# Attention with decay and a feed-forward layer on one core: the places of operands in on-chip memory

## The chip, the core and the metric

The kernel runs on one core of a Trainium2 chip. The core has engines that work beside each other: TensorE (PE) multiplies matrices and writes to PSUM, VectorE (DVE) and ScalarE (ACT) do elementwise work and move data between PSUM and the on-chip memory SBUF, GpSimd (POOL) fills tables, and SyncE (SP) issues the transfers (DMAs) here. They wait for each other by semaphores. A product on PE has two instructions: a load of the stationary operand (the weights, 128x128; rows of the profile call it PEld), and the matmul proper, which streams the moving operand through.

The metric is the time of one execution on the device, in microseconds. The median of three runs of the kernel before is 647.0 us (646.7 to 647.45).

## The reference

Two layers, all in float32. The first is attention with decay over 4 batches, 8 heads, 768 positions of 64 features, computed in blocks with a state that is carried on:

```
intra = (q_b k_b^T) * Dmask          # Dmask[i,j] = lam^(i-j) where i >= j, else 0
out   = intra v_b + (q_b * lam^(i+1)) kv_state
kv_state = lam^block * kv_state + (k_b * lam^(block-1-j))^T v_b
```

Its output, 3072 tokens of 512 features, goes through a feed-forward layer:

```
h   = maximum(x @ w_in, 0)           # 512 -> 2048
out = (h * h) @ w_out                # 2048 -> 512
```

## The kernel before

*Tiles.* The 24 chunks of 128 positions (4 batches, 6 chunks each) are grouped three at a time into eight tiles of 384 tokens. For each tile and each of 16 blocks f of 128 hidden features, `ffn` (L498) does one step. The first product (`mm1`, L507) multiplies x by a block of w_in: 12 matmuls of 384 columns. ACT takes the relu (L521); the square is taken on ACT alone for the first two tiles (L523, L524), on ACT and DVE for the others (L526, L527); DVE makes the low part gl (L528). The second product (`mm2`) has nine matmuls of 512 columns: six at L513 and L514 with gh, three at L516 with gl.

*Two parts of a number.* Where the products run on the type float32r, a value is held as a high part and a low part, each of that type: xh and xl, wih and wil, woh and wol, gh and gl, and a product is the sum of three. In the first product the stationary operand is wih or wil and the moving one xh or xl. In the second gh or gl is stationary, in pieces of 128 columns, and woh or wol moves.

*Attention.* The chunks of the first three tiles go through `unit_plain` (L302): products in float32 from tiles pnt. The others go through `unit_split` (L380): products in float32r, with operands ab, ka, ss, vv and pp made from tiles pkt by ACT and DVE. Plain work ends before split work begins: the buffers of the plain chunks and of the preparation of weights (kinds in `EARLY`, L154) are given back, and the buffers in `LATE` are laid over the same memory (`late`, L209).

*What sets the order.* Nothing is scheduled at run time. Every operation is entered with `plan.op`: its engine, an assumed duration in microseconds, a key, and what it depends on. `Plan.order` plays all engines through with these durations and so writes out one order for each engine; each engine then works through its list and waits on semaphores. The durations of the products stand at L518, L530, L531 and L537. SP is one such list too: loads of pnt, of weights (L276), of pkt (L401) and the stores (L549).

*Where the buffers lie.* SBUF tiles are allocated one after the other (L191 to L207), each rounded up to 32 bytes of a partition. Counted in rows of 512 bytes, all buffers from gh to xl1 begin 128 bytes into a row, since their sizes are whole rows and small constants stand before them. Then come five small tables, lam, ej, ec, wdec and lc (L194 to L198), which take 64 + 32 + 32 + 32 + 32 = 192 bytes. So everything behind them, rdec, mask, all weights, and the early and late buffers, begins 320 bytes into a row. lam holds the decays, wdec and lc their powers, ej and ec the exponents; they are filled at the start (`start_tables`, L221), and flip, a table for one product at the start, already lies in the first 128 columns of the last g buffer.

## Time and profile before

| what | value |
|---|---|
| median of three runs | 647.0 us (646.7 to 647.45) |
| profiled execution, its own time | 646.68 us |
| its span, first to last instruction | 644.9 us |
| mean granted clock of TensorE | 0.999 |
| PE busy | 635.6 us (99%) |
| weight loads (PEld) busy | 569.3 us (88%) |
| DVE busy | 470.9 us (73%) |
| ACT busy | 372.4 us (58%) |
| POOL busy | 5.5 us (1%) |

The profiled execution is one run with the hardware profiler on. Busy times of different engines overlap, so they don't add up to the span. Matmuls are pipelined: each shows a length of 337 ns (384 columns) or 395 to 400 ns (512 columns), while the next one starts long before that has passed, so the distance from start to start says more than the length. In the timeline, equal instructions that follow each other are merged into one row with a count. Idle time in brackets is that of the engine before the row, and behind the arrow stands what ended it.

### The profile page before, as it was taken

The numbers are of one execution on the slowest core, as the hardware profiler recorded it, in microseconds if no ns is written. First come the engines' busy times: TensorE is split into PE (matmuls) and PEld (weight loads), VectorE is DVE, ScalarE is ACT, GpSimd is POOL, SyncE is SP. The second block draws the span as 40 slices with busy tenths as digits, with TensorE's granted clock in tenths as the row PEclk, the third lists the DMA queues.
The fourth block names the chain that finished last, engine by engine and source line by source line (L and its number), as shares of the span: only waits on it lengthen the run. The fifth ranks groups of instructions, "written<-read, shape, count | busy, mean of one in ns | idle before, by whom it ended". The sixth has DMA issues, their size and how long they took to land.

```text
span 644.9 us, 9615 instructions
## 1 busy us (share of the span) xinstructions
PE 635.6 (99%) x3620; PEld 569.3 (88%) x3620; DVE 470.9 (73%) x1046; ACT 372.4 (58%) x863; POOL 5.5 (1%) x15
## 2 busy tenths in 40 slices
PE   8999999999899999999999999999999999999997
PEld 6788989888789998899989999899899898999996
DVE  4999999744348998589975999759995798742222
ACT  6996777755445666366654657556664567532221
POOL 2000000000000000000000000000000000000000
PEclk9999999999999999999999999999999999999999
DMA  7725555430221221231202122121130121010001
GB/s 290 266 99 180 181 189 201 164 115 10 91 85 62 66 90 42 99 99 49 99 1 98 55 94 98 50 100 49 50 99 33 67 99 50 1 50 1 0 1 49
DMA packets 15165, 56.71 MB, mean 88 GB/s; under 512 B 1808, under 2 KB 1808, under 8 KB 15120
## 3 DMA queue, kind: packets, MB, share of 16 engines
q1 hardware_dynamic: 15120, 56.11, 25.4%
q8 instruction: 28, 0.46, 0.3%
q14 instruction: 17, 0.14, 0.1%
HBM read 49.81 MB, written 6.29 MB: 87 GB/s over the span
## 4 chain that ended last, share of the span: by engine, by line
PE 82%; DVE 13%; ACT 3%; DMA 1%; issue 1%; SPq 0%; ACTq 0%
PE h L507 35%; PE bank L516 13%; PE bank L513 12%; PE bank L514 12%; PE bank L473 2%; PE bank L472 2%; PE bank L430 2%; DVE xr L485 1%; DVE g L527 1%; PE bank L450 1%; PE bank L317 1%; DVE gl L528 1%; DVE s L438 1%; PE bank L369 1%; DVE ka L418 1%; DVE ab L416 1%
## 5 line engine op out<-in xcount | busy, mean ns | idle before, releaser
L513 PE MATMUL bank<-woh,gh 128*128 128x512 f32 x384 | 152.1, 396 | 0.0
L514 PE MATMUL bank<-wol,gh 128*128 128x512 f32 x384 | 151.6, 395 | 0.0
L521 ACT ACTIVATE g<-h 128x384 f32<-128x384 f32 x128 | 62.8, 491 | 128.6 <-PE h L507 128.4
L516 PE MATMUL bank<-woh,gl 128*128 128x512 f32 x384 | 111.7, 400 | 0.6 <-DVE gl L528 0.2
L507 PE MATMUL h<-xh,wih 128*128 128x384 f32 x512 | 110.3, 337 | 1.8 <-ACT g L521 1.8
L527 DVE TENSOR_TENSOR g<-g 128x384 f32<-128x384 f32 x96 | 53.5, 557 | 79.5 <-ACT gh L526 79.1
L507 PE MATMUL h<-xh,wil 128*128 128x384 f32 x512 | 109.8, 336 | 0.0
L507 PE MATMUL h<-xl,wih 128*128 128x384 f32 x512 | 109.4, 336 | 0.0
L507 PEld LDWEIGHTS h<-xh,wih 128*128 128x128 f32 x512 | 89.8, 188 | 6.6 <-ACT g L521 2.2
L507 PEld LDWEIGHTS h<-xh,wil 128*128 128x128 f32 x512 | 90.6, 188 | 0.0
L507 PEld LDWEIGHTS h<-xl,wih 128*128 128x128 f32 x512 | 90.4, 188 | 0.0
L516 PEld LDWEIGHTS bank<-woh,gl 128*128 128x128 f32 x384 | 70.1, 188 | 19.5 <-DVE gl L528 4.1
L513 PEld LDWEIGHTS bank<-woh,gh 128*128 128x128 f32 x384 | 72.2, 188 | 13.4 <-issue 0.2
L514 PEld LDWEIGHTS bank<-wol,gh 128*128 128x128 f32 x384 | 72.2, 188 | 13.1
L528 DVE TENSOR_TENSOR gl<-g,gh 128x384 fp32r<-128x384 f32 x128 | 71.1, 556 | 16.7 <-ACT gh L524 13.5
L526 ACT ACTIVATE gh<-g 128x384 fp32r<-128x384 f32 x96 | 50.5, 526 | 2.5
L479 ACT COPY z<-bank 128x256 f32<-128x256 f32 x60 | 22.3, 372 | 38.4 <-PE bank L473 35.9
L480 DVE TENSOR_TENSOR z<-bank,z 128x256 f32<-128x256 f32 x60 | 25.0, 423 | 14.1 <-ACT z L479 12.7
L473 PE MATMUL bank<-pp,vv 128*128 128x256 f32 x120 | 29.8, 281 | 0.0
L472 PE MATMUL bank<-ab,ss 128*128 128x256 f32 x120 | 29.7, 281 | 0.0
L437 ACT COPY s<-bank 128x256 f32<-128x256 f32 x60 | 20.0, 373 | 14.2 <-PE bank L430 13.9
L485 DVE TENSOR_TENSOR xr<-z,zl 64x256 f32<-64x256 f32 x60 | 25.1, 418 | 2.0 <-ACT zl L481 1.0
(78 smaller groups left out, 775.1 us busy)
## 6 DMA issues: line engine op xcount, KB each, us to landing
pkt<-pk SPq DMA_DIRECT2D x30, 768.0 KB, 4.4
st<-w SPq DMA_DIRECT2D x32, 512.0 KB, 3.4
pnt<-pn SPq DMA_DIRECT2D x18, 512.0 KB, 4.5
out<-ob SPq DMA_DIRECT2D x23, 256.0 KB, 2.2
out<-z SPq DMA_DIRECT2D x1, 256.0 KB, 2.0
lam<-lamx SPq DMA_DIRECT2D x1, 6.0 KB, 1.7
```

Source lines behind the costliest of these rows:

```text
L472: nc.tensor.matmul(y4[:, n], at(ss)[:, n, h].rearrange("p t d -> p (t d)"), at(ab)[:, i], start=n == 0, stop=False, skip_group_check=True)
L473: nc.tensor.matmul(y4[:, n], at(vv)[:, i].rearrange("p t d -> p (t d)"), at(pp)[:, i], start=False, stop=True, skip_group_check=True)
L480: zo.append(add("DVE", 0.36, 2, lambda h=h, part=part: nc.vector.tensor_tensor(out=at(z)[:, h], in0=part(0), in1=at(z)[:, h], op=ALU.add), ...
L485: nc.vector.tensor_tensor(out=at(xr)[half(h)], in0=at(z)[0:64, h], in1=at(zl)[:, h], op=ALU.add)
L507: nc.tensor.matmul(at(h)[:, 0:N], wt[:, cc, :], xt[:, cc, :], start=k == 0, stop=k == 3 * NCC - 1)
L513: nc.tensor.matmul(at(os_[j]), at(gh)[:, sl], woh[f], start=f == 0, stop=False)
L514: nc.tensor.matmul(at(os_[j]), at(gh)[:, sl], wol[f], start=False, stop=False)
L516: nc.tensor.matmul(at(os_[j]), at(gl)[:, sl], woh[f], start=False, stop=f == NF - 1)
L521: orr = plan.op("ACT", 0.45, key, lambda: nc.scalar.activation(at(g), at(h)[:, 0:N], AF.Relu), [o1], [h, g])
L526: ogh = plan.op("ACT", 0.47, key, lambda: nc.scalar.activation(at(gh), at(g), AF.Square), [orr], [g, gh])
L527: og = plan.op("DVE", 0.48, key, lambda: nc.vector.tensor_tensor(out=at(g), in0=at(g), in1=at(g), op=ALU.mult), [orr, ogh], [g])
L528: ogl = plan.op("DVE", 0.48, key, lambda: nc.vector.tensor_tensor(out=at(gl), in0=at(g), in1=at(gh), op=ALU.subtract), [og, ogh], [g, gh, gl])
```

## The change

The tables lam, ej and ec move into unused columns of the last g buffer (from column 128 on, behind flip). wdec and lc move behind the weights. So rdec, mask and all weights begin 128 bytes into a row, as the buffers before them do. wdec and lc take 64 bytes, so the early buffers begin at 192. The late pool starts with a tile `space` of 448 bytes, and the late buffers begin at 128 again. In the planner the durations of the products are written anew, the list of plain chunks is written by its count of chunks (nine, the same chunks), and one start key changes for tiles of which none is split (no effect).

```diff
-N_PLAIN = 3
-PLAIN = [bc for t in TILES[:N_PLAIN] for bc in t]
-SPLIT = [bc for t in TILES[N_PLAIN:] for bc in t]
+N_PLAIN = 9
+PLAIN, SPLIT = CHUNKS[:N_PLAIN], CHUNKS[N_PLAIN:]
...
-    lam = const.tile([P, 12], F32, name="lam")
-    ej = const.tile([P, H], F32, name="ej")
-    ec = const.tile([P, NP], F32, name="ec")
-    wdec = const.tile([P, H], F32, name="wdec")
-    lc = const.tile([P, NP], F32, name="lc")
     rdec = const.tile([P, NP, C], F32, name="rdec")
 
     flip, zero = tiles["g"][-1][:, 0:P], tiles["ob"][-1]
+    lam, ej, ec = (tiles["g"][-1][:, P + 16 * i:P + 16 * i + n] for i, n in enumerate((H + NP, H, NP)))
...
+    wdec = const.tile([P, H], F32, name="wdec")
+    lc = const.tile([P, NP], F32, name="lc")
     make(phase.enter_context(tc.tile_pool(name="early", bufs=1)), EARLY)
 
     def late():
         phase.close()
-        make(ctx.enter_context(tc.tile_pool(name="late", bufs=1, reuse_waits="tile")), LATE)
+        pool = ctx.enter_context(tc.tile_pool(name="late", bufs=1, reuse_waits="tile"))
+        pool.tile([P, 112], F32, name="space")
+        make(pool, LATE)
...
-        o1 = plan.op("PE", 2.09, key, mm1, list(ready) + list(wo[0]), [x, h], [last_mm.get((ti, 1))])
+        o1 = plan.op("PE", 2.085, key, mm1, list(ready) + list(wo[0]), [x, h], [last_mm.get((ti, 1))])
...
-            o2 = plan.op("PE", 1.41, key + 1.9, lambda: [mm2(0, j) for j in range(NT)], [ogh] + list(wo[1]), [gh] + os_, [last_mm.get((ti, 2))])
-            last_mm[ti, 2] = o3 = plan.op("PE", 0.7, key + 1.9, lambda: [mm2(1, j) for j in range(NT)], [ogl], [gl, gh] + os_, [o2])
+            o2 = plan.op("PE", 1.37, key + 1.9, lambda: [mm2(0, j) for j in range(NT)], [ogh] + list(wo[1]), [gh] + os_, [last_mm.get((ti, 2))])
+            last_mm[ti, 2] = o3 = plan.op("PE", 0.685, key + 1.9, lambda: [mm2(1, j) for j in range(NT)], [ogl], [gl, gh] + os_, [o2])
...
-                elif ti < N_PLAIN:
+                elif (b, c) in PLAIN:
...
-                    f0 = 0.5 if ti > 2 else 2.0
+                    f0 = 0.5 if ti > 2 else 1.0
```

The new durations make the planner write another order. Two engines are shown at the place where plain chunks end and split ones begin, and POOL at the start. In the names the number behind the last underscore is a running number of the tile and shifts by itself; the number before it is the buffer.

PE before, from the last product of a plain chunk with the state (L366) on; woh10 is the second weight block of step 10, wih11 to wih13 the first ones of the steps that follow:

```order
L366 MATMUL bank2_63<-pnt1_174,diag1_0_179 128x128 x2
L369 MATMUL bank2_63<-s1_1_89,vd1_91 64x128 x4
L516 MATMUL bank1_62<-woh10_148,gl1_73 128x512
L516 MATMUL bank0_61<-woh10_148,gl1_73 128x512
L516 MATMUL bank5_66<-woh10_148,gl1_73 128x512
L507 MATMUL h1_68<-xh1_97,wih11_117 128x384 x4
L507 MATMUL h1_68<-xl1_98,wih11_117 128x384 x4
L507 MATMUL h1_68<-xh1_97,wil11_133 128x384 x4
L507 MATMUL h0_67<-xh1_97,wih12_118 128x384 x4
L507 MATMUL h0_67<-xl1_98,wih12_118 128x384 x4
L507 MATMUL h0_67<-xh1_97,wil12_134 128x384 x4
L507 MATMUL h1_68<-xh1_97,wih13_119 128x384 x4
```

PE now, from the same product on:

```order
L366 MATMUL bank2_63<-pnt1_171,diag1_0_176 128x128 x2
L369 MATMUL bank2_63<-s1_1_89,vd1_91 64x128 x4
L513 MATMUL bank1_62<-woh11_144,gh0_69 128x512
L514 MATMUL bank1_62<-wol11_160,gh0_69 128x512
L513 MATMUL bank0_61<-woh11_144,gh0_69 128x512
L514 MATMUL bank0_61<-wol11_160,gh0_69 128x512
L513 MATMUL bank5_66<-woh11_144,gh0_69 128x512
L514 MATMUL bank5_66<-wol11_160,gh0_69 128x512
L516 MATMUL bank1_62<-woh11_144,gl0_72 128x512
L516 MATMUL bank0_61<-woh11_144,gl0_72 128x512
L516 MATMUL bank5_66<-woh11_144,gl0_72 128x512
L513 MATMUL bank1_62<-woh12_145,gh2_71 128x512
```

Before, three second products and then the first products of steps 11, 12 and 13 follow. Now the nine second products of step 11 and the nine of step 12 come next, and after them the first products of steps 13 and 14 and then the second ones of step 13; the first products of steps 11 and 12 stand ahead of the L366.

ACT before, at the first casts from pkt to ab (L415); L521 is the relu, and the first one behind the casts takes the h of step 11:

```order
L521 ACTIVATE g2_77<-h0_67 128x384
L523 ACTIVATE g2_77<-g2_77 128x384
L524 CAST gh1_70<-g2_77 128x384
L375 CAST xh0_95<-xr0_93 128x2x128
L375 CAST xh0_95<-xr1_94 128x2x128
L415 CAST ab0_1646<-pkt0_1644 128x4x128
L417 CAST ka0_1648<-pkt0_1644 128x512
L406 CAST ss0_0_1653<-hold0_80 64x2x64 x2
L415 CAST ab1_1647<-pkt1_1645 128x4x128
L521 ACTIVATE g0_75<-h1_68 128x384
L422 CAST vv0_1649<-vd0_90 128x4x64
L523 ACTIVATE g0_75<-g0_75 128x384
```

ACT now, at the same casts; the first relu behind them takes the h of step 13:

```order
L521 ACTIVATE g1_76<-h0_67 128x384
L523 ACTIVATE g1_76<-g1_76 128x384
L524 CAST gh2_71<-g1_76 128x384
L375 CAST xh0_95<-xr1_94 128x2x128
L415 CAST ab0_1670<-pkt0_1668 128x4x128
L417 CAST ka0_1672<-pkt0_1668 128x512
L406 CAST ss0_0_1677<-hold0_80 64x2x64 x2
L415 CAST ab1_1671<-pkt1_1669 128x4x128
L422 CAST vv0_1673<-vd0_90 128x4x64
L406 CAST ss1_0_1678<-hold1_81 64x2x64 x2
L521 ACTIVATE g0_75<-h1_68 128x384
L523 ACTIVATE g0_75<-g0_75 128x384
```

The casts from pkt stand two steps later among the relus, and the cast to vv and the second pair to ss now stand ahead of the relu.

POOL at the start, before and then now, with what each instruction waits for:

```order
L229 AFFINE_SELECT g_77<-g_77 128x128 [waits DVE_49]
L230 AFFINE_SELECT mask<-mask 128x128 [waits DVE_49]
L233 MEMSET diag_0_177 128x256
L233 MEMSET diag_1_178 128x256
L233 MEMSET diag_0_179 128x256
L233 MEMSET diag_1_180 128x256
L235 TENSOR_TENSOR wdec<-lam,ej 128x8 [waits DMAHW0_49,Pool_49]
```

```order
L229 AFFINE_SELECT g_77<-g_77 128x128 [waits DVE_49]
L230 AFFINE_SELECT mask<-mask 128x128 [waits DVE_49]
L233 MEMSET diag_0_174 128x256
L233 MEMSET diag_1_175 128x256
L233 MEMSET diag_0_176 128x256
L233 MEMSET diag_1_177 128x256
L235 TENSOR_TENSOR wdec<-g_77 128x8 [waits DMAHW0_49,Pool_49]
```

The sequence and the waits are the same; pow (L235) reads lam and ej out of g.

## Rows read from the trace of the kernel before

**Rows 1.** The page: busy time, share of the span, instructions.
```profile
PE 635.6 (99%) x3620; PEld 569.3 (88%) x3620; DVE 470.9 (73%) x1046; ACT 372.4 (58%) x863; POOL 5.5 (1%) x15
```

**Rows 2.** Table by stretch: stretch, length, busy time by engine, granted clock, DMA.
```profile
80.00:120.00 40.00, 40.00 (x202) 36.04 (x201) 39.55 (x79) 31.55 (x66) 0.53 (x1) 1.00 0.63 215
...
200.00:240.00 40.00, 40.00 (x228) 36.72 (x226) 37.11 (x89) 25.62 (x60) 0.00 (x0) 1.00 0.23 79
...
560.00:600.00 40.00, 40.00 (x205) 35.95 (x204) 14.86 (x28) 11.51 (x23) 0.00 (x0) 1.00 0.06 20
```

**Rows 3.** Waits: who waited for whom, us in total, times, longest.
```profile
PEld bank L516 <- DVE gl L528: 4.1, 11, 0.6
...
PE h L507 <- ACT g L521: 1.8, 1, 1.8
```

**Rows 4.** Timeline of PE late in the kernel: start, length, instruction.
```profile
578.03 0.39 PE L513 MATMUL bank<-woh,gh 128*128 128x512 f32 x1
...
580.13 0.39 PE L513 MATMUL bank<-woh,gh 128*128 128x512 f32 x1
...
582.23 0.86 PE L507 MATMUL h<-xh,wih 128*128 128x384 f32 x4
...
586.39 0.39 PE L513 MATMUL bank<-woh,gh 128*128 128x512 f32 x1
```

**Rows 5.** Groups by line: shapes and count, busy time and mean ns, idle.
```profile
L514 PE MATMUL bank<-wol,gh 128*128 128x512 f32 x384 | 151.6, 395 | 0.0
...
L507 PE MATMUL h<-xh,wih 128*128 128x384 f32 x512 | 110.3, 337 | 1.8 <-ACT g L521 1.8
...
L514 PEld LDWEIGHTS bank<-wol,gh 128*128 128x128 f32 x384 | 72.2, 188 | 13.1
```

**Rows 6.** Timeline, all engines, a second product and the next load.
```profile
636.55 0.39 PE L513 MATMUL bank<-woh,gh 128*128 128x512 f32 x1
636.56 0.19 PEld L514 LDWEIGHTS bank<-wol,gh 128*128 128x128 f32 x1
```

**Rows 7.** Timeline of PE in split attention: its value products.
```profile
240.77 0.28 PE L472 MATMUL bank<-ab,ss 128*128 128x256 f32 x1
...
241.71 0.39 PE L513 MATMUL bank<-woh,gh 128*128 128x512 f32 x1
```

**Rows 8.** Groups by line on ACT: three casts of 512 columns.
```profile
L441 ACT CAST pp<-s 128x512 fp32r<-128x512 f32 x30 | 18.6, 621 | 12.2 <-DVE s L439 11.7
...
L415 ACT CAST ab<-pkt 128x512 fp32r<-128x512 f32 x30 | 18.7, 624 | 3.3 <-DMA pkt<-pk 3.3
...
L286 ACT CAST woh<-m 128x512 fp32r<-128x512 f32 x16 | 9.9, 621 | 5.1 <-DVE m L284 4.9
```

**Rows 9.** Timeline, all engines, at the start.
```profile
0.80 0.38 SPq L222 DMA_DIRECT2D lam<-lamx  x1
...
3.20 1.64 POOL L235 TENSOR_TENSOR wdec<-lam,ej 128x8 f32<-128x8 f32 x1
```

**Rows 10.** Timeline, all engines, from plain to split chunks.
```profile
158.82 0.60 PE L366 MATMUL bank<-pnt,diag 128*128 128x128 f32 x4
...
159.50 0.81 SPq L401 DMA_DIRECT2D pkt<-pk  x2
...
159.95 0.96 PE L516 MATMUL bank<-woh,gl 128*128 128x512 f32 x3
...
163.94 0.62 ACT L415 CAST ab<-pkt 128x512 fp32r<-128x512 f32 x1 [3.01 <-DMA pkt<-pk]
...
165.84 0.62 ACT L415 CAST ab<-pkt 128x512 fp32r<-128x512 f32 x1 [0.24 <-DMA pkt<-pk]
...
166.37 0.48 ACT L521 ACTIVATE g<-h 128x384 f32<-128x384 f32 x1
...
166.90 0.96 PE L507 MATMUL h<-xh,wih 128*128 128x384 f32 x4 [1.83 <-ACT g L521]
...
168.10 0.51 ACT L524 CAST gh<-g 128x384 fp32r<-128x384 f32 x1
```

More of the change, by code (lines that the diff above doesn't have):

```diff
@@ L536, in ffn @@
             for j in range(NT):
-                o3 = plan.op("PE", 0.7, key + 1.9 + j * 0.01, lambda j=j: [mm2(0, j), mm2(1, j)], [ogh, ogl] + list(wo[1]), [gh, gl] + os_[j:], [o3])
+                o3 = plan.op("PE", 0.69, key + 1.9 + j * 0.01, lambda j=j: [mm2(0, j), mm2(1, j)], [ogh, ogl] + list(wo[1]), [gh, gl] + os_[j:], [o3])
                 done.append(o3)
```

## The prediction

> **What bounds the kernel now.** I read the page's busy times first: TensorE (PE) is busy 99% of the span, DVE 73%, ACT 58% [rows 1]. A busy PE is not yet a PE at its peak, so I went on to the table by stretch. [...] DVE fills 39.55 of 40 us while weights are prepared and 37.11 of 40 where chunks of attention are made beside the products, and only 14.86 of 40 near the end [rows 2]. Then the waits, for who holds PE up: PE itself waited 1.8 us for h, and its weight loads 4.1 us for gl, in 644.9 us [rows 3]. So the time is the number of products times the distance from one to the next, and the change can act on that distance.
>
> I took the distances from the late stretch, where nothing but the two large products runs. From 582.23 to 586.39 PE starts two groups of 12 first products (L507): 4.16 us / 24 = 173.3 ns each. From 578.03 to 580.13 it starts nine second products (L513, L514, L516): 2.10 us / 9 = 233.3 ns each [rows 4]. [...]
>
> **The change part by part.**
>
> *Places.* Each product reads two things at a time: the moving operand, and the weights of the next product. The load for L514 starts at 636.56, right behind the matmul of L513 at 636.55 [rows 6]. Before, the moving x of a first product lies 128 bytes into a row of 512 and the weights that load beside it (wih, wil) 320 bytes in; in a second product it is the other way round (woh, wol at 320, gh, gl at 128). After the change all six lie at 128. [...]
>
> [...]
>
> [...] The planner's costs (L518, L530, L531) say what a group of products takes. Before they are 2.09 for 12 first products, 1.41 for six second ones and 0.70 for three; the rows give 2.08, 1.40 and 0.70 [rows 4]. So these three entries are durations to within 0.01 us. The change writes 2.085, 1.37 and 0.685. That they are again durations, those of the new places, is an assumption, for no run shows it. If they are: 0.005 us + 0.04 us + 0.015 us less in each of 1536 / 12 = 128 groups [rows 5], so 0.6 us from the first products and 5.1 + 1.9 = 7.0 us from the second. I take 7.6 us. [...]
>
> [...]
>
> *Other readers of these tiles.* ACT writes 128x512 in 621 ns both to woh at 320 and from s at 128 to pp at 320, 624 ns from pkt to ab [rows 8]. So an ACT operand's place shows at most 3 ns. On the 863 instructions of ACT [rows 1] that is 2.6 us of an engine that is busy 58% of the span, which PE covers. I take ACT, and DVE and the transfers by the same measure, at zero; uncovered it would be 2.6 us to either side. The plain chunks' operands (pnt) go from 320 to 192, still beside vd and s1 at 128: zero.
>
> *Tables in g.* lam, ej and ec now lie in the last g buffer. The order shows the same waits on POOL, and the first steps keep their place: pow runs at 3.20 us, after lam was issued at 0.80 [rows 9]. The region has its next writer only when relu fills that g, long after. Zero, both ways, since the same instructions wait for the same transfers.
>
> *The late buffers.* pkt1 now also lies over the old pnt3, so its load waits for one more transfer. That one landed before the plain products that read it, and they all stand ahead of the L366 for which both loads wait anyway. Behind it on SP stand the stores of the second tile, whose buffers are filled later still. Zero.
>
> *The order at the hand-over.* With new costs the planner writes another order. Before, both loads of pkt are issued at 159.50, behind the last plain product (L366, 158.82). ACT reaches the cast of pkt, finds nothing, and sits idle 3.01 us until 163.94. The relu for h stands behind two casts to ab, one to ka and two to ss, and starts only at 166.37. PE has run out of h buffers: it waits 1.83 us and goes on at 166.90 [rows 10]. In the new order two more relus stand ahead of the casts, and the last L366 is followed by 18 second products and 24 first ones before PE needs the gh that is made behind the casts. From L366's end at about 159.4 on the old clock that is 0.5 (to the L516 at 159.95) + 18 x 0.233 + 24 x 0.173 = 8.9 us. ACT has the same pieces to do as before between the first cast of pkt and the cast to that gh (two casts to ab, one to ka, two groups to ss, one to vv, relu, square, cast to gh), only in another sequence. Before, that cast to gh starts at 168.10 and takes 0.51 [rows 10]: 9.2 us after the same point. So PE waits some 0.4 us, with what it takes to pass the word on, instead of 2.2 (that gap counted from matmul to matmul). Gain 1.8 us; ends: 2.2 if the wait goes, -0.5 if ACT is later still.
>
> *The order elsewhere* shifts which group stands beside which. The waits that can change there are the 4.1 us of weight loads for gl [rows 3]. Part of those stay hidden under the running matmul. I take zero, with 1.5 us to either side.
>
> **Sum.** On the profiled execution (646.68 us, span 644.9, so 1.8 around it): 646.68 - 7.6 - 1.8 = 637.3. The median of the runs is 0.3 above the profiled one, so 637.6 us. DVE stays under PE: where it is busy 37.11 of 40 us, 40 becomes about 39.4. In the stretch with 39.55 of 40 [rows 2] cover is thin. There the new order has PE's own work on the second tile to fill gaps. If DVE holds that stretch to its old length, 80 us x 1.2% = 1 us of the gain is lost, which is inside the range.
>
> **The rivals.**
> [...]
> *Places don't matter.* The distances stay at 173.3 and 233.3 ns and only the order moves: 647.0 - 1.8 = 645.2, between 643.5 and 647.5. [...] This covers the case that the change does not do what it says. [...]
> *The same place is worse.* [...] It decides from a mean loss of 0.67 ns a product on (1.8 us / 2688), say first products at 174.5 ns with the second unchanged. Against it: the planner's new costs are lower.
> *The new order waits.* The hand-over gets longer (+0.5) and new gl waits cost 1.5 us, while the products gain as forecast: 647.0 - 7.6 + 2.0 = 641.4.
>
> **How the numbers follow.** Forecast 0.62 (its own range 634.5 to 641); new order waits 0.08; one amount for each load 0.12; places don't matter 0.08; worse 0.10. A measurement here tells 0.2%, 1.3 us, from no change. Faster: 0.62 + 0.08 + 0.12, and 0.04 of the case that places don't matter: 0.86. Same: its other 0.04. Slower: 0.10. The range leaves out "worse" but for its mild half, and the lower half of the one-amount case: 631.0 to 648.0.
>
> **What would show it.** In the late stretch, where no order enters, I look for 12 first products in 2.08 us or 2.07, nine second ones in 2.05 instead of 2.10. If the second products stay at 233 ns, the term of the places is wrong and only the order moved. [...] At the hand-over: PE's gap near 165 us shrinks to under 1 us and moves behind the first products of step 14. POOL's pow still at 3.2 us would confirm the tables. A gap in PE before 120 us that was not there would mean that DVE's cover is gone.

## The result, and the profile after

The changed kernel takes 641.34 us (median of four runs, 640.98 to 641.44); the kernel before took 646.93 in the same set. The ratio is 0.9911, with a 95% interval of 0.9894 to 0.9929. A second set gives 641.21 us and 0.9903 (0.9887 to 0.9918). The forecast was 637.6: the sign was right and the time lies inside the whole range (631.0 to 648.0), but just outside the range of the forecast's own account (634.5 to 641), and 3.7 us of the forecast gain of 9.4 did not come.

The 47 executions of the kernel before that ran beside the versions below lie in two groups, 25 from 646.5 to 647.8 us and 22 from 648.1 to 649.0; the mean granted clock of TensorE is 0.999 or 1.000 in the first group and 0.996 or 0.997 in 20 of the 22 others. A profile with the same order shows below where the clock falls. The profiled run of [rows 1 to 10] is of the first group, and sums start from it.

The busy times and the chain of waits on the page of the changed kernel:

```profile
PE 631.4 (99%) x3620; PEld 569.4 (89%) x3620; DVE 469.4 (73%) x1046; ACT 372.1 (58%) x863; POOL 5.5 (1%) x15
...
PE 93%; ACT 3%; DMA 2%; issue 0%; DVE 0%; SPq 0%; ACTq 0%
```

Beside [rows 1] PE has 4.2 us less of busy time and the other engines did the same work. PE is still the bound, now for 93% of the chain.

The late stretch, TensorE's timeline of the changed kernel, answers to [rows 4]:

```profile
573.04 0.39 PE L513 MATMUL bank<-woh,gh 128*128 128x512 f32 x1
...
575.12 0.39 PE L513 MATMUL bank<-woh,gh 128*128 128x512 f32 x1
...
577.16 0.87 PE L507 MATMUL h<-xh,wih 128*128 128x384 f32 x4
...
579.27 0.85 PE L507 MATMUL h<-xh,wih 128*128 128x384 f32 x4
...
581.35 0.39 PE L513 MATMUL bank<-woh,gh 128*128 128x512 f32 x1
```

The row at 579.27 is where the second dozen of first products begins. The first nine second products after the turn from 384 to 512 columns take 2.08 us (231.1 ns each), the next nine 2.04 (226.7 ns). The first products, which took 2.08 us a dozen before, take 2.11 in the dozen behind a turn and 2.08 in the next. Two steps, 18 and 24 products, take 8.31 us where before took 8.36 (578.03 to 586.39). So both lengths lose something after each turn, and I had counted on the settled distance all along.

The hand-over, answering to [rows 10]: the timeline of the changed kernel, SP's queue, ACT and PE:

```profile
164.06 0.81 SPq L401 DMA_DIRECT2D pkt<-pk  x2
...
168.47 0.62 ACT L415 CAST ab<-pkt 128x512 fp32r<-128x512 f32 x1 [2.96 <-DMA pkt<-pk]
...
171.93 0.49 ACT L521 ACTIVATE g<-h 128x384 f32<-128x384 f32 x1
...
172.25 0.86 PE L507 MATMUL h<-xh,wil 128*128 128x384 f32 x4
...
173.01 0.51 ACT L524 CAST gh<-g 128x384 fp32r<-128x384 f32 x1
...
173.57 0.50 PE L513 MATMUL bank<-woh,gh 128*128 128x512 f32 x1 [0.47 <-ACT gh L524]
```

ACT stands at the cast of pkt as long as before (2.96 us against 3.01), and its relu (171.93) still comes behind all the casts, but PE has 18 second and 24 first products to do meanwhile. Its gap from matmul to matmul was 2.17 us and is 0.81, behind the first products of step 14 and not ahead of them, as forecast.

What I had set at zero and was not zero are the weight loads that wait for gl. The waits of the weight loads in the changed kernel:

```profile
PEld bank L516 <- DVE gl L528: 2.7, 11, 0.4
```

Before, they were 4.1 us [rows 3]. Five of these waits stand out before, near 250, 327, 406, 483 and 542 us, with gaps of 496 to 548 ns between the matmuls, one for each tile of split attention; none of the five is in the changed kernel. The timeline of the kernel before at the first of them, DVE, the first second product and the load that waits:

```profile
248.08 0.56 DVE L527 TENSOR_TENSOR g<-g 128x384 f32<-128x384 f32 x1
248.44 0.39 PE L513 MATMUL bank<-woh,gh 128*128 128x512 f32 x1
248.56 0.42 DVE L420 TENSOR_TENSOR vd<-pkt,wdec 128x256 f32<-128x256 f32 x1
...
248.89 0.68 DVE L442 TENSOR_TENSOR pp<-s,pp 128x512 fp32r<-128x512 f32 x1
...
249.49 0.55 DVE L528 TENSOR_TENSOR gl<-g,gh 128x384 fp32r<-128x384 f32 x1
...
250.10 0.53 PEld L516 LDWEIGHTS bank<-woh,gl 128*128 128x128 f32 x3 [0.54 <-DVE gl L528]
```

And the same place in the changed kernel:

```profile
246.03 0.56 DVE L527 TENSOR_TENSOR g<-g 128x384 f32<-128x384 f32 x1
...
246.51 0.68 DVE L442 TENSOR_TENSOR pp<-s,pp 128x512 fp32r<-128x512 f32 x1
...
247.11 0.55 DVE L528 TENSOR_TENSOR gl<-g,gh 128x384 fp32r<-128x384 f32 x1
...
247.58 0.42 DVE L420 TENSOR_TENSOR vd<-pkt,wdec 128x256 f32<-128x256 f32 x1
247.72 0.53 PEld L516 LDWEIGHTS bank<-woh,gl 128*128 128x128 f32 x3 [0.25 <-DVE gl L528]
```

Before, the product of pkt and a table (L420) stands between the square and gl, so gl ends after the sixth second product has begun, and PE stops. Now it stands behind gl. This holds for the first four of the five. At the fifth L420 stood behind gl already, and the square began late (540.39, against the L513 at 540.36); there the new order has PE do two products of the split attention ahead of those with gl, which fills the wait:

```profile
537.14 0.39 PE L430 MATMUL bank<-ab,ka 128*128 128x256 f32 x2
```

### The profile page after: what moved, and what is told of

It reads as the page before. It is cut to its first block, busy times and chain, and to the rows that moved or that the text cites. A ratio compares the mean times of both kernels' runs of the same rounds, so it can differ in the third digit from the quotient of the medians.

```text
span 639.6 us, 9612 instructions
## 1 busy us (share of the span) xinstructions
PE 631.4 (99%) x3620; PEld 569.4 (89%) x3620; DVE 469.4 (73%) x1046; ACT 372.1 (58%) x863; POOL 5.5 (1%) x15
## 4 chain that ended last, share of the span: by engine, by line
PE 93%; ACT 3%; DMA 2%; issue 0%; DVE 0%; SPq 0%; ACTq 0%
PE h L507 41%; PE bank L516 14%; PE bank L513 14%; PE bank L514 14%; PE bank L473 2%; PE bank L430 2%; PE bank L472 2%; PE bank L450 2%; DMA pnt<-pn 2%; DMA pkt<-pk 1%; PE bank L317 1%; PE bank L369 1%; ACT vd L328 1%; ACT diag L356 1%; PE bank L340 0%
## 5 line engine op out<-in xcount | busy, mean ns | idle before, releaser
L513 PE MATMUL bank<-woh,gh 128*128 128x512 f32 x384 | 151.1, 394 | 0.7 <-ACT gh L524 0.7
L521 ACT ACTIVATE g<-h 128x384 f32<-128x384 f32 x128 | 62.9, 492 | 139.3 <-PE h L507 138.9
L516 PE MATMUL bank<-woh,gl 128*128 128x512 f32 x384 | 110.4, 396 | 0.0
L527 DVE TENSOR_TENSOR g<-g 128x384 f32<-128x384 f32 x96 | 53.4, 557 | 75.7 <-ACT gh L526 75.2
L516 PEld LDWEIGHTS bank<-woh,gl 128*128 128x128 f32 x384 | 70.0, 188 | 16.8 <-DVE gl L528 2.7
L513 PEld LDWEIGHTS bank<-woh,gh 128*128 128x128 f32 x384 | 72.1, 188 | 14.3 <-ACT gh L524 1.1
L528 DVE TENSOR_TENSOR gl<-g,gh 128x384 fp32r<-128x384 f32 x128 | 71.1, 556 | 14.5 <-ACT gh L524 11.1
```

The source lines that it names most:

```text
L513: nc.tensor.matmul(at(os_[j]), at(gh)[:, sl], woh[f], start=f == 0, stop=False)
L516: nc.tensor.matmul(at(os_[j]), at(gl)[:, sl], woh[f], start=False, stop=f == NF - 1)
L521: orr = plan.op("ACT", 0.45, key, lambda: nc.scalar.activation(at(g), at(h)[:, 0:N], AF.Relu), [o1], [h, g])
L527: og = plan.op("DVE", 0.48, key, lambda: nc.vector.tensor_tensor(out=at(g), in0=at(g), in1=at(g), op=ALU.mult), [orr, ogh], [g])
L528: ogl = plan.op("DVE", 0.48, key, lambda: nc.vector.tensor_tensor(out=at(gl), in0=at(g), in1=at(gh), op=ALU.subtract), [og, ogh], [g, gh, gl])
```

## The experiments

*The two halves.* First the places without the planner's new costs, so with the order of before; then the costs and their order alone, with the buffers of before.

Places alone (the whole diff but for these four entries, which stay as before):

```diff
         o1 = plan.op("PE", 2.09, ...
             o2 = plan.op("PE", 1.41, ...
             last_mm[ti, 2] = o3 = plan.op("PE", 0.7, ...
                 o3 = plan.op("PE", 0.7, ...
```

> The change's buffers, with the planner's durations of before, so the order of before. Theory: both halves of the change act; the places took some 3.5 us from the second products (mean distance 233.0 to 229.8 ns, 1152 of them) and gave 0.9 us back on the first ones (173.6 to 174.2 ns, 1536), so this kernel takes 647 - 2.6 = 644.3 us. Rival 1, the places do it all: 641.3 us. Rival 2, the order does it all: 647 us. In the late stretch, second products at 226.7 to 231 ns by the theory, 233.3 ns by rival 2.

Measured: 646.01 us (644.64 to 646.69), ratio 0.997 (0.996 to 0.998). Its runs come in two groups as well: six from 644.6 to 645.9 with a granted clock of 1.000, six from 646.1 to 646.7 with 0.996 or 0.997; the profiled one is of the second. The timeline of TensorE in it, behind the hand-over:

```profile
166.87 1.04 PE L507 MATMUL h<-xh,wih 128*128 128x384 f32 x4 [1.87 <-ACT g L521]
167.71 1.48 PE L507 MATMUL h<-xl,wih 128*128 128x384 f32 x4
168.99 1.48 PE L507 MATMUL h<-xh,wil 128*128 128x384 f32 x4
170.27 0.63 PE L513 MATMUL bank<-woh,gh 128*128 128x512 f32 x1
```

From 167.71 to 170.27 eight products take 320 ns each instead of 174; the granted clock is 0.88 from 160 to 170 us and 0.95 from 170 to 180 us here, and 1.00 from 160 to 170 us before. Group against group (medians 645.3 and 646.5, before 646.7 and 648.3) the places alone are worth 1.4 to 1.8 us: not the 7.6 of the forecast, and less than the 2.6 expected here.

Order alone:

```diff
-        o1 = plan.op("PE", 2.09, ...
+        o1 = plan.op("PE", 2.085, ...
-            o2 = plan.op("PE", 1.41, ...
-            last_mm[ti, 2] = o3 = plan.op("PE", 0.7, ...
+            o2 = plan.op("PE", 1.37, ...
+            last_mm[ti, 2] = o3 = plan.op("PE", 0.685, ...
-                o3 = plan.op("PE", 0.7, ...
+                o3 = plan.op("PE", 0.69, ...
```

> The buffers of before, with the planner's durations of the change, so its order. Theory: the order is worth about 3 us (the gap at the hand-over 2.2 to 0.8 us, fewer waits for gl), so 643.9 us, with second products at 233.3 ns in the late stretch. Rival 1, the places do it all: 647 us. Rival 2, the order does it all: 641.3 us.

Measured: 643.17 us (643.04 to 643.33), ratio 0.9931 (0.9917 to 0.9945). So the order is worth 3.5 us against the first group (646.7), about twice the 1.8 of the forecast, and no run has the fall of the clock (0.998 to 1.000). Its hand-over gap is 0.75 us, and the weight loads' waits for gl have halved:

```profile
PEld bank L516 <- DVE gl L528: 2.2, 10, 0.3
```

*What a place costs.* A kernel of products alone, in runs of 24 at one length, with the moving operand shifted against the stationary one. In a row of its table by stretch stand the stretch, its length, the busy time of PE and of the weight loads with their counts in brackets (one or two matmuls more than the 24 that start in the stretch), DVE and POOL, the granted clock, and the DMA.

```diff
+        for d in range(0, 512, 64):
+            for n in (512, 384, 256):
+                run(0, d, n)
+        for so, mo in ((192, 192), (192, 0), (192, 384)):
+            for n in (512, 384, 256):
+                run(so, mo, n)
+        for _ in range(3):
+            run(0, 0, 384, 24)
+            run(0, 0, 512, 18)
```

The arguments of `run` are the place of the stationary operand, that of the moving one, the columns and, at the end, the count of products.

> No part of the computation, zeros as output: runs of 24 matmuls with nothing else on the core, at 512, 384 and 256 columns; the stationary operand stays and the moving one is shifted against it by 0, 64, 128 to 448 bytes; then both at 192; at the end three times 24 of 384 columns and 18 of 512 at the same place. Theory, one amount for each load where the places are the same: 226.7, 173.3 and 120 ns at 0 (13.3 ns over the columns), and 233.3, 173.3 and 118 ns at 192; both at 192 as both at 0. Rival, the loss goes with the columns: at 0 the loss at 512 columns is twice that at 256. Rival, places don't matter: the same distances at every shift. For the switch between 384 and 512 columns the theory expects the first products after each switch to be off their steady distance, as in the late stretch of the changed kernel.

Eight of its stretches, in order: no shift at 512, 384 and 256 columns, a shift of 64 bytes at the same three, a shift of 192 at 512, and at 384 columns the stationary operand at 192 with the moving one at 384:

```profile
15.81:21.25 5.44, 5.44 (x26) 4.50 (x24) 0.00 (x0) 0.00 (x0) 1.00 0.93 351
21.25:25.43 4.18, 4.18 (x25) 4.18 (x24) 0.00 (x0) 0.00 (x0) 1.00 0.02 4
25.43:28.30 2.87, 2.87 (x25) 2.87 (x25) 0.00 (x0) 0.00 (x0) 1.00 0.00 0
28.30:33.90 5.60, 5.60 (x26) 4.54 (x25) 0.00 (x0) 0.00 (x0) 1.00 0.00 0
33.90:38.06 4.16, 4.16 (x25) 4.15 (x24) 0.00 (x0) 0.00 (x0) 1.00 0.00 0
38.06:40.89 2.83, 2.83 (x26) 2.83 (x25) 0.00 (x0) 0.00 (x0) 1.00 0.00 0
...
53.53:59.12 5.59, 5.59 (x26) 4.52 (x25) 0.00 (x0) 0.00 (x0) 1.00 0.00 0
...
147.03:151.27 4.24, 4.24 (x25) 4.24 (x24) 0.00 (x0) 0.00 (x0) 1.00 0.00 0
```

The settled distances, read from the starts inside each run:

| shift, bytes | 512 columns | 384 | 256 |
|---|---|---|---|
| 0 (and 256) | 226.7 ns | 173.3 | 120.0 |
| 64 (and 320) | 233.3 | 173.3 | 117.8 |
| 128 (and 384) | 232.5 | 175.7 | 118.8 |
| 192 (and 448) | 233.3 | 174.5 | 113.3 |
| 192, stationary at 192 | 233.3 | 176.7 | 117.7 |

Where the last row doesn't say otherwise, the stationary operand lies at 0. Moved to 192 as well, shifts of 0 and 64 read as before, but 192 doesn't (384 and 256 columns): so the shift decides most of the distance and not all of it. The expectation had 173.3 and 118 at 192.

Three things follow. With the stationary operand at 0 the settled distances repeat after 256 bytes, not 512 (at 512 columns 226.7 ns at shifts of 0 and 256, 233.3 at 64 and 320). At the same place the three distances lie on one line: 53.3 and 53.4 ns for 128 columns more, so 0.417 ns a column, and 13.3 ns besides at all three lengths (226.7 - 213.3, 173.3 - 160.0, 120.0 - 106.7): one amount for each product, which I call the loss. And the kernel before fits in: its first products had x at 128 and weights at 320, a shift of 64 modulo 256, and settled at 173.3 already; its second ones had a shift of 192, 233.3 ns. So the first products had nothing to gain. In the turns that the kernel makes, a run at the same place first takes 170, 175, 178, 185, 176, 181 ns at 384 columns and 229, 234, 236, 224, 231, 235, 229, 232, 231 at 512 before it settles, some 26 and 41 ns more in all than as many settled ones.

*Only the first products at the same place* (the second ones' weights go back to 320):

```diff
     wil = [const.tile([P, NCC, P], F32R, name=f"wil{f}") for f in range(NF)]
+    const.tile([P, 48], F32, name="shift")
     woh = [const.tile([P, DM], F32R, name=f"woh{f}") for f in range(NF)]
...
-        pool.tile([P, 112], F32, name="space")
+        pool.tile([P, 64], F32, name="space")
```

> The changed kernel, with woh and wol alone put back to 320 bytes into a row (a spacer of 192 bytes before them); wih and wil stay at 128, the order stays. Theory: the place acts on the second products and hurts the first ones a little: second products back at 233 ns in the late stretch, first ones at 174, time 641.3 + 3.5 = 644.8 us. Rival, the place of the first product's weights is what gained: time stays at 641.3 us, second products stay below 230 ns.

Measured: 643.46 us (643.24 to 643.61), ratio 0.9935 (0.992 to 0.9951), against 643.17 with no place changed. The first products' place gains nothing. It costs 0.3 us here (sums of the first products' distances 267.8 and 267.6 us), less than the 0.9 us that the changed kernel's sums had led me to expect; the 644.8 of the expectation lies 1.3 us above the measured time.

*All pairs of places in the kernel's own turn*: 24 first, then 18 second products, on constant data.

```diff
+        for b in SHIFTS:
+            for a in SHIFTS:
+                for _ in range(2):
+                    group(a, b)
```

SHIFTS is 0, 32, and so on to 224; a moves wih and wil, b moves woh and wol.

> Only PE's products on constant data, in the turn of the late stretch (24 first products, then 18 second ones), with the first products' weights moved by a and the second ones' moving operand moved by b, a and b in steps of 32 bytes from 0 to 224; its output is zeros. One number for each pair: the time of 24 + 18. From the map: b at 0 gives 226.7 ns in the steady part and some 43 ns more after the turn, so 4.12 us for the 18; b at 64, 128 or 192 gives 233 ns, 4.19 to 4.20. The first products give 4.16 us without a loss after the turn (a at 192, which is before's place), 4.19 with it (a at 0), 4.21 at a of 64 or 128. So the theory that each product's loss hangs on its own two places alone has the lowest pair at (a 192, b 0), 8.28 us, against 8.31 at (0, 0) and 8.36 at (192, 192). Rival: what is lost after a turn hangs on the place of the products before it too; then the pair that is lowest lies elsewhere, and the table is not the sum of a row and a column. Steps of 32: if the memory is read in pieces of 64 bytes, they read as their neighbours; if in pieces of 32, they lie between or above them.

The time of 24 + 18 in nanoseconds, from the starts in its trace, at six of the 64 pairs, each in its last pass:

| first, a | second, b | 24 first | 18 second | sum |
|---|---|---|---|---|
| 0 | 0 (the change) | 4186 | 4129 | 8315 |
| 192 | 192 (before) | 4167 | 4195 | 8362 |
| 0 | 192 | 4172 | 4188 | 8360 |
| 192 | 0 | 4165 | 4125 | 8290 |
| 192 | 64 | 4159 | 4128 | 8287 |
| 32 | 0 | 4168 | 4116 | 8284 |

The pair (192, 0) in its timeline, from the first product to the first of the next turn:

```profile
123.87 0.86 PE L35 MATMUL h<-xh,wih 128*128 128x384 f32 x4
...
128.03 0.40 PE L41 MATMUL bank<-woh,gh 128*128 128x512 f32 x1
...
132.16 0.69 PE L35 MATMUL h<-xh,wih 128*128 128x384 f32 x3
```

The three lowest pairs lie within 6 ns, and the change's own pair is 25 to 31 ns above them. In the pass before, these four give 8280 (192, 0), 8284 (192, 64), 8294 (32, 0) and 8306 (0, 0): the order among the three is not settled, the distance to the change's pair is 12 ns at the least. The second products are low at b = 0 (4102 to 4129) and, against the map, nearly so at 64 (4126 to 4137, but for one of 4199); elsewhere they take 4176 to 4221. The table is a sum of row and column only roughly: with b at 192 moving a from 192 to 0 adds 5 ns to the 24, with b at 0 it adds 21, so for the first products the place of the second ones before them counts. Nor do the two places settle it alone: at eight of the 64 pairs the 24 first products take 65 to 78 ns more in one pass than in the other, as at a = 64, b = 128 (4236, then 4161). Steps of 32 bytes don't read as their neighbours: at b = 32 the 18 second products take 4176 ns or more, at 0 4129 or less, and at 64 4137 or less but for the one.

*Only the second products at the same place* (the first ones' weights at 320 as before):

```diff
-    wih = [const.tile([P, NCC, P], F32R, name=f"wih{f}") for f in range(NF)]
-    wil = [const.tile([P, NCC, P], F32R, name=f"wil{f}") for f in range(NF)]
     woh = [const.tile([P, DM], F32R, name=f"woh{f}") for f in range(NF)]
     wol = [const.tile([P, DM], F32R, name=f"wol{f}") for f in range(NF)]
+    const.tile([P, 48], F32, name="shift")
+    wih = [const.tile([P, NCC, P], F32R, name=f"wih{f}") for f in range(NF)]
+    wil = [const.tile([P, NCC, P], F32R, name=f"wil{f}") for f in range(NF)]
...
-        pool.tile([P, 112], F32, name="space")
+        pool.tile([P, 64], F32, name="space")
```

> The changed kernel with the first products' weights (wih, wil) back at 320 bytes, where they were before, and only the second ones' (woh, wol) at 128. If the second products' place is all that the change of places gives, and the first products at the same place lose some 27 ns after each turn, as the map has it, this keeps the second products' gain and takes that loss away: 64 turns of 24 first products by 0.027 us is 1.7 us at most, by the sums of distances in the changed kernel's trace (268.6 us against 267.6 with the old places) 0.9 us: 640.4 us, with 639.6 as the lower end. Rival: the loss after a turn belongs to the turn and not to the first products' place, or goes over to the second products: 641.3, as the changed kernel.

Measured: 640.06 us (639.93 to 640.17), ratio 0.9883 (0.9863 to 0.9903). This version beats the change by 1.15 us. TensorE's timeline in its late stretch (the line numbers are one higher in this version):

```profile
571.92 0.40 PE L514 MATMUL bank<-woh,gh 128*128 128x512 f32 x1
...
576.04 0.86 PE L508 MATMUL h<-xh,wih 128*128 128x384 f32 x4
...
580.20 0.40 PE L514 MATMUL bank<-woh,gh 128*128 128x512 f32 x1
```

The 18 second products still take 4.12 us, and the 24 first ones 4.16 instead of 4.19: 8.28 us for two steps, as the pairs have it. So the first products at the same place cost 1.15 us where the second ones lie there too, and 0.3 us where those lie at 320: the two places don't simply add up.

> The changed kernel once more, on the chip on which the others of this set run: 641.3 us, and between 640.9 and 641.7. Both theories expect the same; it is the measure for the others.

The changed kernel beside it, once more: 641.21 us (640.93 to 642.05), the measure for the set.

*The hand-over alone.* On the kernel before, one more dependence in the plan, so that the planner no longer takes pkt to be there early (`plain_end` holds the value products of the plain chunks):

```diff
-        load = add("SP", 2.6, -8, ..., [o_start], [t], "load")
+        load = add("SP", 2.6, -8, ..., [o_start, plain_end[-1]], [t], "load")
```

> The kernel before in places and in the planner's costs. One dependence is added in the plan alone: the loads of pkt are entered as ready only behind the last plain value product. So the casts of pkt move behind the next relu and its casts on ACT (and their counterparts on DVE), and one group of 12 first products moves behind nine second ones on PE; nothing else moves. Theory of the hand-over: PE's wait of 2.2 us near 165 us comes from ACT, which stands at the cast of a pkt that has not landed, ahead of the relus. Then the wait goes but for some 0.4 us: 1.8 us less than the kernel before where its clock stays at the upper level (646.6), so 644.8; and since the fall of the clock near 168 us followed that wait, it goes too, and the runs no longer come in two groups (646.6 and 648.3). Rival: the casts are then late for the split products, and PE waits for ab or ss instead, as long: 646.6. Rival of the clock: its fall has nothing to do with the wait; then runs at +1.7 us stay.

Measured: 645.15 us (644.88 to 645.98), ratio 0.9964 (0.9951 to 0.9976); no run of seven lies at 646 or above, and the granted clock is 0.999 or 1.000 in all of them. That is 1.5 us below the first group of before (646.7), where 1.8 was expected. ACT and PE in its timeline:

```profile
163.68 0.49 ACT L521 ACTIVATE g<-h 128x384 f32<-128x384 f32 x1 [0.94 <-PE h L507]
...
164.76 0.51 ACT L524 CAST gh<-g 128x384 fp32r<-128x384 f32 x1
164.87 0.86 PE L507 MATMUL h<-xh,wil 128*128 128x384 f32 x4
165.18 0.62 ACT L415 CAST ab<-pkt 128x512 fp32r<-128x512 f32 x1
...
165.57 0.39 PE L513 MATMUL bank<-woh,gh 128*128 128x512 f32 x1
```

The relu runs ahead of the cast of pkt, and PE goes from its first products to the second ones without a gap. So the wait was the cast's place on ACT, and the fall of the clock goes with the wait: the profiles of three kernels that keep it show the fall (granted clock from 160 to 170 us 0.88 with places alone, 0.91 and 0.93 in two below), that of the kernel before keeps it and shows none (1.00), and no profile of a kernel without it has the fall (1.00 in each).

*Which number makes the order.* On the buffers of before, three choices of the planner's costs. I had a rule by then, in the first of these expectations: read the hand-over, and count the places where two other entries stand between a square and its gl on DVE (the four of the kernel before are the four waits of this kind above).

```diff
         2.085 for 2.09                       (first cost alone)
         1.37, 0.685, 0.69 for 1.41, 0.7, 0.7 (second costs alone)
         1.45, 0.72, 0.72 for 1.41, 0.7, 0.7  (costs up)
```

> The kernel before with one planner's cost of the change alone: 2.085 for 2.09 us of a first product's group, the second ones' costs as before. Theory: an order's price is read at two kinds of place. At the hand-over it is 1.5 us when the casts of pkt stand ahead of the relu that PE needs next. In each tile of attention it is some 0.27 us when both the table for vd and the low part of pp stand on DVE between a square and its gl (in the kernel before four times, in the changed one once, as ka and pp). This order has the hand-over of the changed kernel (two relus ahead of the casts), and such a pair on DVE four times, and once ka and pp: 646.6 - 1.5 = 645.1, as with the hand-over alone, with no fall of the clock. Rival: the gain of the order comes from costs nearer to the places' durations; then 0.005 of 2.09 us gives next to nothing: 646.6, with a part of the runs at 648.3.

> The kernel before with the other costs of the change alone: 1.37, 0.685 and 0.69 for 1.41, 0.70 and 0.70, the first ones' 2.09 as before. This is nearly all of the change in the planner's numbers. Theory: its order has the old hand-over (the casts of pkt ahead of the relu), and two entries on DVE between a square and its gl ten times: nothing is gained at the hand-over, and up to six more waits of 0.27 us: 646.6 to 648.2 in the runs with the clock at its upper level, with falls of the clock in part of them. Rival (it is these costs that make the better order): 643.2, as with all the costs of the change.

> The kernel before with the second products' costs moved the other way, away from what they take: 1.45, 0.72 and 0.72 us. Theory: its order has the old hand-over (with its wait and, in part of the runs, the fall of the clock), but on DVE a pair between a square and its gl once only, where before has four: 646.6 - 3 x 0.27 = 645.8 with the clock at its upper level, some 1.7 more without. Rival (costs further from the durations make a worse order): 647 or more with the clock at its upper level.

| order | hand-over gap | waits for gl | time (median, range) | ratio (95%) |
|---|---|---|---|---|
| before | 2.17 us | 4.1 us (11) | 646.7, profiled | |
| hand-over alone | none | 4.3 (12) | 645.15 (644.88 to 645.98) | 0.9964 (0.9951 to 0.9976) |
| first cost alone | 0.77 | 4.9 (12) | 645.58 (645.57 to 646.09) | 0.997 (0.9958 to 0.9982) |
| second costs alone | 2.18 | 1.3 (5) | 645.43 (644.97 to 647.01) | 0.9974 (0.9963 to 0.9985) |
| all of the change's | 0.75 | 2.2 (10) | 643.17 (643.04 to 643.33) | 0.9931 (0.9917 to 0.9945) |
| costs up | 2.20 | 6.7 (15) | 650.17 (649.9 to 650.31) | 1.004 (1.0027 to 1.0052) |

The waits of the weight loads with the first cost alone, then with the second costs alone, then with costs up:

```profile
PEld bank L516 <- DVE gl L528: 4.9, 12, 0.6
```

```profile
PEld bank L516 <- DVE gl L528: 1.3, 5, 0.4
```

```profile
PEld bank L516 <- DVE gl L528: 6.7, 15, 0.7
```

The hand-over was read rightly from all three orders: a change of 0.005 us in one cost moves it, and the 0.04 us in the others doesn't. The runs with the second costs alone lie in two groups, 645.0 to 645.6 (granted clock 1.000) and 646.7 to 647.0 (0.997), as the old hand-over has it. Those with costs up don't: 649.9 to 650.3 at clocks from 0.996 to 1.000, so there the price of the fall isn't shown. The rule for gl failed: ten pairs on DVE cost less than before's four, and the order with one pair waited most. What decides is when gl ends, and the row of DVE with costs up shows another way to be late, with no vd in between:

```profile
239.75 0.58 DVE L410 TENSOR_TENSOR ss<-hold,ss 64x128 fp32r<-64x128 f32 x2
...
240.34 0.39 PE L513 MATMUL bank<-woh,gh 128*128 128x512 f32 x1
...
240.36 0.56 DVE L527 TENSOR_TENSOR g<-g 128x384 f32<-128x384 f32 x1
...
240.84 0.69 DVE L442 TENSOR_TENSOR pp<-s,pp 128x512 fp32r<-128x512 f32 x1
...
241.44 0.55 DVE L528 TENSOR_TENSOR gl<-g,gh 128x384 fp32r<-128x384 f32 x1
...
242.05 0.74 PE L516 MATMUL bank<-woh,gl 128*128 128x512 f32 x2 [0.15 <-DVE gl L528]
```

Here the square itself begins with the first second product, at 240.36, as at the fifth wait of the kernel before; at the first of those it begins 0.36 us ahead of it (248.08, against the L513 at 248.44). The rival, that costs nearer to the durations make the better order, isn't borne out either: on the old buffers the second products take 1.40 and 0.70, and the costs below that (1.37, 0.685) gave the least waiting for gl.

*Both together*: only the second products at the same place, the change's costs, and the dependence of the hand-over kernel.

```diff
-        load = add("SP", 2.6, -8, ..., [o_start], [t], "load")
+        load = add("SP", 2.6, -8, ..., [o_start, plain_end[-1]], [t], "load")
```

> Only the second products at the same place (the first ones' weights at 320 as before), the changed kernel's costs, and the loads of pkt entered in the plan as ready behind the last plain value product. Theory: at the hand-over the 0.5 us that PE still waited for gh go to 0.1 or so, since the relu and its casts stand one cast further ahead on ACT, and DVE's order has no pair between a square and its gl where it had one: 640.06 - 0.4 - 0.2 = 639.5. Rival: the wait at the hand-over stays, since ACT has the same pieces to do up to that gh; then 639.9 to 640.1.

Measured: 639.12 us (639.0 to 639.42), ratio 0.987 (0.9854 to 0.9887), the fastest version: 2.1 us below the change (641.21), and 0.9 below the version before it, where 0.6 was expected. The table by stretch has PE busy throughout where 9.53 of 10 us stood in the changed kernel:

```profile
170.00:180.00 10.00, 10.00 (x52) 9.03 (x51) 3.01 (x6) 5.00 (x10) 0.00 (x0) 1.00 0.00 0
```

## Why the prediction was right or wrong

| term | forecast | measured | from |
|---|---|---|---|
| places, second products | -7.0 us | -3.1 | sum of distances, order alone 270.35, change 267.28 |
| places, first products | -0.6 | +1.0 | the same sums, 267.60 and 268.57 |
| hand-over | -1.8 | -1.4 | gap, before 2.17 us, order alone 0.75 |
| order elsewhere | 0 | -1.9 | waits for gl, before 4.1, order alone 2.2 |

The order's terms are taken between the kernel before and the order alone, those of the places between the order alone and the change. Together they are -5.4, as between the profiled runs (646.68 and 641.31); a part of the waits of loads is hidden under running products (before, the loads of L516 waited 4.1 us for gl, and the page has 0.6 us of idle PE ahead of those products), so the sum is not as exact as it looks. The order is worth more than the places, where the forecast had it four to one the other way. That the time still lies in the whole range is in part luck: 5.5 us of the places' gain did not come, and 1.5 us more came from the order. The figure of the prediction that is nearest, 641.4, belongs to the rival "The new order waits", whose waits didn't come.

*Places.* That a gain lies in the second products was right; its size was not. The step that failed is "That they are again durations, those of the new places, is an assumption". The entry 1.37 is 228.3 ns a product, between the 231.1 of the nine behind a turn and the settled 226.7; the mean over the 1121 second products that nothing disturbs is 229.8. A second slip lies in my subtraction. I took the new entries from the old ones (1.41, 2.09) and not from the rows (1.40, 2.08). Against the rows the second products would give 128 x 0.045 = 5.8 us and the first ones a loss of 128 x 0.005 = 0.6, which has the sign that was measured. I read a lowered entry as a gain and passed over the row beside it.

*The rivals.* The range holds a one-amount case, with 0.12, and the mild half of "worse". No run shows an amount for each load, for none leaves the loads out, nor a loss that grows with the columns; what the map shows at the same place is 13.3 ns for each product beside 0.417 ns a column. The eight value products of [rows 7] stand 117.5 ns apart; in the map the first eight at the same place take 118.4 ns each at 256 columns, and only then 120.0. That the eight of [rows 7] were such unsettled ones is not shown. "Places don't matter" falls with the map: 226.7 against 233.3 ns with nothing waited for, and with the moving operand at 192 the settled distance at 512 columns is 233.3 ns where the stationary one lies at 0, and 226.7 where it lies at 192. "The same place is worse" holds for the first products, +1.0 us by distances and 1.15 by time (only 0.3 where the second ones stay at 320), and not for the second; the dozen behind a turn takes 2.11 us (175.8 ns each) and the next 2.08 (173.3). "The new order waits" didn't come: the hand-over gap shrank and the waits for gl fell.

*Hand-over.* Right in place and cause, shown by the dependence alone. The gap that remains was forecast as 0.4 us and is 0.81 from matmul to matmul, of which the profile shows 0.47 as idle.

*Order elsewhere.* Set at zero with 1.5 to either side, on the rows of gl. It came out beyond that end. The five longest waits stood in the trace of before, and at four of them the new order had L420 behind L528, at the fifth two other products on PE; I had read the sum of the waits and not their places. That such waits hang on the order is shown by the three choices of costs; that a count of entries foretells them is not.

*The zeros.* POOL's pow starts at 3.21 us (3.20 before). ACT and DVE take what they took. No gap came up in PE in the early stretch from 40 to 120 us.

Left open: what in the chip makes the loss (no run leaves the weight loads out), why the same pair of places gives two times (4236 and 4161 ns), why a run at one place needs six to nine products to settle after such a turn, and why the 18 second products at a shift of 64 are quicker in the kernel's turn than in the map.

## What to carry to other kernels

Where TensorE is the bound, take the distance from start to start for each length and place, settled and behind a turn apart, before you move buffers: here the same place was worth 3.1 us for one kind of product and cost up to 1.15 for the other. Set a planner's new number against the row of the trace, never against its old number. And a reordering that comes along is a term of its own: look, on each engine that works in order, for what stands ahead of the instruction that TensorE waits for; it gave more here than the change that brought it.

## What the runs showed of the hardware

- The distance between products hangs on the places of moving and stationary operand to each other, by up to 6.6 ns at 512 columns (226.7 to 233.3), 3.4 ns at 384 (173.3 to 176.7) and 6.7 ns at 256 (113.3 to 120.0); with the stationary operand at 0 the settled distances repeat after 256 bytes (226.7 ns at shifts of 0 and 256, 233.3 at 64 and 320). The shift alone doesn't settle it: at a shift of 192 and 384 columns it is 174.5 ns with the stationary operand at 0 and 176.7 with it at 192. At 256 columns the same place is the slowest (120.0 ns, against 113.3 and 117.7 at a shift of 192).
- After a turn between 384 and 512 columns at the same place the first 384s lose some 26 ns in all and the first 512s some 41 (40 to 49 in the pairs).
- The wait of 2.2 us on TensorE is followed, in part of the executions, by a fall of the granted clock (0.88 as the mean from 160 to 170 us with places alone; eight products at 320 ns), which costs some 1.7 us by the two groups of times. Where the profile has PE wait there for 0.6 us or less, the mean granted clock was 0.998 or more in every run.
